# A linear-attention and two-MLP kernel: a new opening order, pairs of units one chunk earlier, a decay written in place, and low halves taken earlier

## The chip, the cores and the metric

One core of one Trainium2 chip runs the whole program in one launch. The metric is the device time of that launch in microseconds (us). TensorE is called PE in the profile (its weight loads PEld), VectorE DVE, ScalarE ACT, GpSimd POOL, SyncE SP. SP issues all DMAs here (SPq in the profile).

## The reference

Inputs are q, k, v and f_logit of shape (4, 8, 768, 48): 4 batches, 8 heads, 768 time steps, 48 features.

```
f = 1 / (1 + exp(-f_logit))
for t in range(768):
    state = f[t][:, None] * state + outer(k[t], v[t])      # 48 x 48 per batch and head
    y[t]  = q[t] @ state
x = y as (3072 tokens, 384)
x = relu(x @ w_in)**2 @ w_out                              # 384 -> 2048 -> 384
h = x @ w_in2 ;  x = (h * tanh(softplus(h))) @ w_out2      # softplus(h) = h above 20
```

All of it is float32.

## The kernel before

**Attention.** Time is cut into 12 pieces of 64 steps, the batches into two pairs: 24 units (`NU`), unit i being piece i // 2 of batch pair i % 2. In a unit the decays are accumulated in log space: `v_min` clips the logits on DVE, `a_exp` and `a_ln` make softplus on ACT, `v_scan` sums along time on DVE, `a_dq` and `a_dk` (ACT) make the queries' and the keys' decay, `v_q` (twice) and `v_k` multiply them in on DVE. Then `m_a` multiplies keys with queries on PE, `v_mask` cuts the result on DVE, `m_t` and `a_kn` turn the keys, `m_y` makes the output, `m_u` and `v_s` the next state, `a_x` and `v_x` split the output into a high and a low part for the MLP (block b of 512 tokens is units 4b to 4b+3). From unit 10 on, units run in pairs: `quarters_a` stands for `m_a` of both, `quarters_u` for `m_u` of the pair before, `v_turn` (DVE) and `a_turn` (8 small copies on ACT) for the turning.

**MLPs.** Each has 6 blocks of 512 tokens and 16 hidden chunks of 128. A float32 product is three fp32r products of high and low parts: `l1` (line 330) is 9 matmuls of 512 columns into one PSUM tile h, `l2` (line 341) 9 matmuls into the three accumulators a0 to a2. Between them ACT takes relu, square and the high half `gh` (`act_a`), DVE the low half `gl` (`act_b`, line 354). At the last chunk of a block `evac` copies the three accumulators out, two on ACT (line 363) and one on DVE (line 361).

**Weights.** They come as 64-bit floats and are rebuilt into float32 halves. For each of the first MLP's 16 chunks `load_w` fetches 768 KB, ACT does `w_abs` and `w_hi`, DVE `w_shift`, `w_top`, `w_low` and `w_lo` (lines 252, 255, 258, 280). The second MLP's weights go the same way beside the middle of the first one (`w2_...`), through DRAM.

**PSUM.** The pool `hps` has five buffers that take turns. `l1`, `m_a`, `m_t`, `m_y`, `m_u` take one each, a `quarters_u` two and a `quarters_a` two. An `l1` can't start before the reader of the tile that had its buffer is done.

**What sets the order.** Instructions stand on their engine in the order in which Python calls them. The opening, up to MLP chunk 18, is a list written out by hand, `START`. It also holds fillers, `m_warm n`, matmuls whose result nobody reads. Behind it a planner sets the order: `put(s, prio, f, ...)` files a step under MLP chunk s, and chunk by chunk the steps are called by rising prio. In a chunk i there are `act_a` of chunk i-1 (5), the attention's steps (9 to 33), `act_b` of i-1 (32 before), `do_l1` of i (100), `quarters_u` and `quarters_a` (110, 111), `do_l2` of i-2 (120). A block's `evac` belongs to the `do_l2` of its last chunk, so it is called in chunks 17, 33, 49, 65 and 81.

**DMA.** SP issues loads in the order of the list and waits at one whose buffer is still in use. Sizes: decay logits alone 256 KB, keys and queries 512 KB, all three 768 KB, values two DMAs of 128 KB, a weight chunk 768 KB. Units 2 to 5 borrow the buffers of weight chunks 15 to 12 for their inputs (`early`).

Of the kernel before, what the change touches and what calls it, by code (L numbers as in the profile page):

```python
# [36 lines left out]
START = """
m_warm 14; load_j 0; v_min 0; a_exp 0; load_j 1; load_j 2; load_j 3; a_ln 0; v_min 1; a_exp 1; v_scan 0; a_ln 1;
load_f 0; load_f 1; v_min 2; v_scan 1; a_dq 0; v_min 3; a_dk 0; v_k 0; a_exp 2; a_dq 1; v_q 0 1; v_q 0 0; a_dk 1;
load_v 0; load_w 0; a_ln 2; a_exp 3; eye_kn 0; load_v 1; load_f 2; m_t 0; m_warm 2; v_end 1; v_k 1; v_q 1 1; load_v 2;  # L40
v_scan 2; a_ln 3; load_f 3; v_end 0; v_q 1 0; m_a 0; m_warm 5; v_scan 3; v_mask 0 0; w_abs 0; v_mask 0 1; m_a 1;
m_warm 4; a_dq 2; a_dk 2; v_mask 1 1; load_v 3; a_dq 3; v_mask 1 0; m_y 0; a_kn 0; load_w 1; w_shift 0; a_dk 3; v_q 2
0; m_t 1; m_warm 2; w_top 0; eye_kn 1; v_q 2 1; load_w 2; m_y 1; m_warm 3; v_q 3 0; v_k 3; v_k 2; v_q 3 1; w_low 0;
a_x 0; m_u 0; a_kn 1; v_s 0 0; m_a 2; w_abs 1; v_x 0; load_w 3; v_mask 2 0; m_u 1; v_s 1 0; v_s 0 1; w_shift 1; m_a 3;
m_t 3; v_mask 2 1; w_hi 0; a_kn 3; m_t 2; m_warm 1; m_y 2; a_kn 2; v_s 1 1; v_mask 3 1; v_mask 3 0; m_warm 1; m_y 3;
m_warm 1; w_lo 0; w_top 1; load_w 4; w_abs 2; a_x 1; v_x 1; w_shift 2; load_f 5; w_low 1; a_x 2; load_w 5; m_warm 6;
load_w 6; v_end 3; a_x 3; v_x 3; v_x 2; w_top 2; do_l1 0; w_hi 1; w_abs 3; load_v 4; w_lo 1; w_low 2; do_l1 1; w_abs
4; w_shift 3; v_min 5; w_hi 2; load_w 7; w_top 3; a_exp 5; w_lo 2; w_shift 4; m_u 3; load_w 8; w_low 3; act_a 0; act_b
0; w_abs 5; w_top 4; w_hi 3; w_shift 5; load_w 9; do_l1 2; act_a 1; w_lo 3; w_low 4; w_hi 4; act_b 1; load_w 11; w_top
5; w_lo 4; w_low 5; v_s 3 0; do_l2 0; do_l1 3; do_l2 1; act_a 2; act_b 2; do_l1 4; w_abs 6; w_hi 5; w_abs 7; w_shift  # L50
6; w_lo 5; w_top 6; do_l2 2; act_a 3; w_abs 8; w_shift 7; w_low 6; load_f 4; a_ln 5; w_hi 6; w_top 7; act_b 3; v_s 3
1; act_a 4; w_lo 6; w_abs 9; do_l1 5; do_l2 3; w_low 7; w_hi 7; load_v 5; act_b 4; w_shift 8; load_f 7; act_a 5;
w_shift 9; load_w 10; do_l1 6; w_top 8; load_f 6; do_l2 4; v_end 2; w_lo 7; w_top 9; w_low 8; act_b 5; act_a 6; w_hi
8; w_abs 11; v_min 4; v_scan 5; w_lo 8; load_v 7; do_l1 7; w_low 9; load_w 14; a_exp 4; do_l2 5; a_ln 4; act_b 6; a_dq
5; w_hi 9; a_dk 5; v_q 5 1; w_abs 10; w_lo 9; v_scan 4; do_l1 8; act_a 7; do_l2 6; v_k 5; a_dq 4; v_q 5 0; act_a 8;
do_l1 9; a_dk 4; w_shift 10; act_b 7; w_top 10; v_q 4 1; m_t 5; v_min 6; w_shift 11; v_k 4; act_a 9; act_b 8; m_a 5;
load_w 12; do_l2 7; v_min 7; m_u 2; v_q 4 0; do_l2 8; w_low 10; a_kn 5; m_a 4; w_top 11; m_t 4; a_exp 7; v_mask 5 0;
w_hi 10; a_ln 7; w_lo 10; v_end 5; v_end 4; w_low 11; act_b 9; w_abs 12; w_hi 11; w_shift 12; v_mask 5 1; w_top 12;
do_l1 10; do_l2 9; w_lo 11; act_a 10; do_l1 11; w_low 12; load_w 13; w_hi 12; w_abs 13; act_b 10; do_l2 10; v_mask 4
1; w_lo 12; v_s 2 0; v_s 2 1; do_l1 12; act_a 11; w_shift 13; v_mask 4 0; w_abs 14; a_exp 6; act_b 11; m_y 5; a_ln 6;  # L60
w_top 13; w_shift 14; a_kn 4; do_l2 11; w_low 13; v_scan 6; w_hi 13; m_y 4; w_lo 13; act_a 12; do_l1 13; v_scan 7;
w_top 14; a_dq 7; act_b 12; a_dk 7; load_w 15; w_low 14; v_q 7 0; m_u 5; v_s 5 0; v_k 7; a_dq 6; v_q 7 1; do_l2 12;
act_a 13; m_u 4; a_dk 6; m_a 7; act_b 13; v_s 4 0; v_q 6 1; w_hi 14; v_q 6 0; do_l2 13; v_s 5 1; load_v 8; v_k 6; v_s
4 1; v_mask 7 1; m_t 7; a_kn 7; w_abs 15; v_mask 7 0; m_a 6; v_mask 6 1; m_t 6; m_y 7; v_mask 6 0; a_kn 6; load_v 6;
a_x 5; m_y 6; a_x 4; w_lo 14; w_shift 15; do_l1 14; v_end 7; w_top 15; w_low 15; v_x 5; load_f 9; w_hi 15; v_x 4;
load_f 8; v_end 6; m_u 7; act_a 14; w_lo 15; m_u 6; v_s 7 0; v_min 8; v_s 7 1; a_exp 8; v_min 9; do_l1 15; a_ln 8; a_x
6; act_b 14; a_x 7; v_scan 8; v_x 6; a_dq 8; v_x 7; v_s 6 1; do_l2 14; a_dk 8; a_exp 9; v_s 6 0; v_k 8; act_a 15; v_q
8 0; act_b 15; a_ln 9; do_l1 16; v_scan 9; m_t 8; v_end 8; act_a 16; load_v 10; do_l1 17; a_dq 9; v_q 8 1; v_q 9 0;
v_end 9; a_dk 9; load_v 9; do_l2 15; a_kn 8; v_q 9 1; do_l1 18; act_b 16; m_a 8; v_mask 8 1; v_mask 8 0; do_l2 16; m_y
8; m_u 8; act_a 17; load_f 10; act_b 17; v_k 9; v_s 8 0; v_s 8 1  # L70
"""
# [880 lines left out]
```

## Time and profile before

| | us |
|---|---|
| median of three runs | 891.13 (889.51 to 891.47) |
| the profiled execution: its time | 892.6 |
| its span, first to last instruction | 890.8 |
| PE busy | 872.1 (98%) |
| DVE busy | 683.9 (77%) |
| ACT busy | 626.6 (70%) |

The granted PE clock is a share of 2.4 GHz; its mean over the span is 0.993. Matmuls are pipelined, so one of 512 columns shows 390 ns while nine of them start within 2.04 us. "Idle before" in a row is the engine's idle time just before it, with what ended it. The span falls into an opening (up to the first `l1` at 38.24 us), the first MLP beside the attention (to about 430 us) and the second MLP.

### The profile page before, as it was taken

What the parts mean: (1) busy time and instruction counts of PE and PEld (TensorE: products, weight loads), DVE (VectorE), ACT (ScalarE), POOL (GpSimd) and SP (SyncE); (2) the same over time, 40 slices, a digit from 0 to 9 for tenths busy, and PEclk for the clock granted to TensorE, in tenths of its full rate; (3) what the DMA queues carried; (4) which work ended last, traced back from release to release, by engine and by line L of the source; (5) the groups of instructions that cost most, each with busy time, mean ns of one, the idle gap of its engine ahead of it and who ended that gap; (6) DMA issues with size and microseconds to landing.
All of it is one profiled execution on the core that took longest, in us unless ns stands there. A gap on an engine that the chain in (4) does not pass through costs nothing.

```text
span 890.8 us, 16582 instructions
## 1 busy us (share of the span) xinstructions
PE 872.1 (98%) x6619; PEld 720.4 (81%) x6619; DVE 683.9 (77%) x1159; ACT 626.6 (70%) x1151; POOL 6.5 (1%) x21
## 2 busy tenths in 40 slices
PE   8899999999999999999999999999999999999996
PEld 8788778887887888788888888888888888888885
DVE  7899986786988897972122888888888888888875
ACT  7598777987987987954544666676666766676664
POOL 2000000000000000000000000000000000000000
PEclk9799999999999999999999999999999999999999
DMA  9962133535466354632653200200200200200001
GB/s 243 387 199 104 51 124 104 181 128 202 147 198 213 131 202 143 202 107 72 212 181 104 71 1 1 71 1 1 71 0 1 71 1 1 71 1 17 20 0 40
DMA packets 30132, 90.80 MB, mean 102 GB/s; under 512 B 3680, under 2 KB 3680, under 8 KB 30048
## 3 DMA queue, kind: packets, MB, share of 16 engines
q1 hardware_dynamic: 30048, 89.67, 30.0%
q8 instruction: 54, 0.88, 0.4%
q14 instruction: 30, 0.25, 0.1%
HBM read 67.63 MB, written 22.02 MB: 101 GB/s over the span
## 4 chain that ended last, share of the span: by engine, by line
PE 83%; DVE 9%; DMA 4%; ACT 2%; issue 1%; SPq 1%; ACTq 0%
PE a L341 40%; PE h L330 40%; DMA r<-in_w_dram 2%; PE y L545 2%; DVE wbit L255 1%; DMA vs<-in_vv_dram 1%; DVE w L280 1%; DVE gl L354 1%; DVE wbit L258 1%; PE aq L478 1%; PE uq L489 1%; DVE vs L571 1%; DVE mv L520 1%; DVE wbit L252 1%; DVE mv L447 0%
## 5 line engine op out<-in xcount | busy, mean ns | idle before, releaser
L330 PE MATMUL h<-x,w 128*128 128x512 f32 x1728 | 424.8, 390 | 3.9 <-ACT r L721 3.5
L341 PE MATMUL a<-gh,w 128*128 128x512 f32 x1146 | 386.4, 392 | 0.0
L330 PEld LDWEIGHTS h<-x,w 128*128 128x128 f32 x1728 | 323.4, 188 | 72.9 <-ACT r L721 4.8
L341 PEld LDWEIGHTS a<-gh,w 128*128 128x128 f32 x1146 | 215.1, 188 | 45.6
L341 PE MATMUL a<-gl,w 128*128 128x512 f32 x573 | 223.4, 390 | 0.5 <-DVE gl L354 0.5
L788 ACT ACTIVATE e<-e 128x512 f32<-128x512 f32 x95 | 60.0, 632 | 116.1 <-DVE e L787 116.1
L341 PEld LDWEIGHTS a<-gl,w 128*128 128x128 f32 x573 | 107.7, 188 | 23.5 <-DVE gl L354 1.8
L354 DVE TENSOR_TENSOR gl<-r,gh 128x512 fp32r<-128x512 f32 x96 | 65.5, 683 | 74.5 <-ACT gh L349 74.0
L787 DVE TENSOR_SCALAR e<-h 128x512 f32<-128x512 f32 x95 | 65.7, 692 | 59.2 <-PE h L330 56.7
L721 ACT ACTIVATE r<-h 128x512 f32<-128x512 f32 x96 | 56.5, 588 | 52.8 <-PE h L330 52.1
L782 ACT ACTIVATE r<-u,cst 128x512 f32<-128x512 f32 x94 | 67.9, 722 | 8.7 <-DVE u L796 2.7
L796 DVE SCALAR_TENSOR_TENSOR u<-e 128x512 f32<-128x512 f32 x95 | 66.0, 694 | 10.0 <-ACT e L788 0.7
L354 DVE TENSOR_TENSOR gl<-g,gh 128x512 fp32r<-128x512 f32 x95 | 65.8, 693 | 0.0
L784 DVE TENSOR_TENSOR e<-h,u 128x512 f32<-128x512 f32 x94 | 64.4, 685 | 0.0
L791 DVE TENSOR_TENSOR g<-e,r 128x512 f32<-128x512 f32 x94 | 64.2, 683 | 0.0
L722 ACT ACTIVATE r<-r 128x512 f32<-128x512 f32 x96 | 60.7, 633 | 3.1
L349 ACT ACTIVATE gh<-r 128x512 fp32r<-128x512 f32 x96 | 60.7, 633 | 3.1
L349 ACT ACTIVATE gh<-g 128x512 fp32r<-128x512 f32 x95 | 60.1, 633 | 3.1 <-DVE g L815 0.8
L783 ACT ACTIVATE r<-r 128x512 f32<-128x512 f32 x94 | 59.4, 632 | 3.0
L500 ACT ACTIVATE kn<-kt 32x256 f32<-32x256 f32 (+1 forms) x104 | 37.6, 362 | 1.4
L432 DVE TENSOR_TENSOR_SCAN es<-es,cap 112x520 f32<-112x520 f32 x24 | 29.6, 1232 | 0.8 <-ACT es L428 0.8
L447 DVE TENSOR_TENSOR mv<-in,eq 48x512 f32<-48x512 f32 x40 | 27.4, 685 | 1.4 <-ACT eq L437 0.6
(116 smaller groups left out, 679.7 us busy)
## 6 DMA issues: line engine op xcount, KB each, us to landing
in<-in_qkf_dram SPq DMA_DIRECT2D x18, 768.0 KB, 6.7
r<-in_w_dram SPq DMA_DIRECT2D x16, 768.0 KB, 10.6
sr<-in_w_dram SPq DMA_DIRECT2D x32, 384.0 KB, 3.7
w2d<-sw SPq DMA_DIRECT2D x32, 384.0 KB, 3.7
w<-w2d SPq DMA_DIRECT2D x32, 384.0 KB, 3.6
vs<-in_vv_dram SPq DMA_DIRECT2D x48, 128.0 KB, 7.3
x2d<-ot SPq DMA_DIRECT2D x18, 256.0 KB, 2.2
x<-x2d SPq DMA_DIRECT2D x6, 768.0 KB, 5.1
```

The lines of the kernel that those rows point to most:

```text
L330: T.matmul(out=ps, lhsT=w[:, k * 128:(k + 1) * 128], rhs=x[:, s, k], start=(i == 0), stop=(i == 8))
L341: T.matmul(out=acc[m], lhsT=w[:, m * 128:(m + 1) * 128], rhs=gx, start=(fc == 0 and i == 0), stop=(fc == FC - 1 and i == 2))
L349: A.activation(out=gh, in_=g, func=AF.Copy)
L354: V.tensor_tensor(out=gl, in0=g, in1=gh.bitcast(F32), op=ALU.subtract)
L722: A.activation(out=r, in_=r, func=AF.Square)
L782: A.activation(out=r, in_=u, func=AF.Ln, bias=two)
L783: A.activation(out=r, in_=r, func=AF.Exp, scale=-1.0)
L784: V.tensor_tensor(out=e, in0=hp, in1=u, op=ALU.mult)
L787: V.tensor_scalar(out=e2, in0=ps, scalar1=20.0, scalar2=None, op0=ALU.min)
L788: A.activation(out=e2, in_=e2, func=AF.Exp)
L791: V.tensor_tensor(out=g, in0=e, in1=r, op=ALU.mult)
L796: V.scalar_tensor_tensor(out=u2, in0=e2, scalar=2.0, in1=e2, op0=ALU.add, op1=ALU.mult)
```

## The change

- `START` is a new list. The step names are the same; their order on every engine, and that of the loads on SP, differs.
- `m_warm n` makes matmuls of up to 512 columns: n counts 128 columns each, as before, but four go into one instruction.
- `a_dq` writes the queries' decay over the unit's decay logits, which `a_exp` has read by then, and no longer into a tile of its own (`eq`).
- Pairs from unit 12 on start one chunk earlier (s is one less), while `m_y`, `a_x` and `v_x` keep their chunk (`end`). `v_s` moves one chunk earlier for all pairs.
- `act_b` has priority 20 in place of 32 outside the last block: ahead of `v_min` (24), `v_scan` (25), `v_q`, `v_k`, `v_end` (26), `v_turn` (27).

```diff
-m_warm 14; load_j 0; v_min 0; a_exp 0; load_j 1; load_j 2; load_j 3; a_ln 0; v_min 1; a_exp 1; v_scan 0; a_ln 1;
+m_warm 20; load_j 0; v_min 0; a_exp 0; load_w 0; load_j 1; load_j 2; a_ln 0; v_scan 0; w_abs 0; v_min 1; a_dq 0;
...
         def a_dq(i):
-            eq = at.tile([112, H, C], F32, tag="eq", name="eq")
+            eq = head(fkq(i)[0])
             A.activation(out=eq, in_=es[i % 3][:, :, 1:], func=AF.Exp, scale=-1.0)
...
         def m_warm(n):
             sm = cap.rearrange("p h t -> p (h t)")
-            for _ in range(n):
-                T.matmul(out=warm[:, 0:128], lhsT=sm[:, 0:128], rhs=sm[:, 0:128])
+            for k in range(n, 0, -4):
+                c = 128 * min(k, 4)
+                T.matmul(out=warm[:, 0:c], lhsT=sm[:, 0:128], rhs=sm[:, 0:c])
...
-                end = s + 4
+                end = 8 * (i // 2) - 11
...
-                    put(s + 9, 12 - odd, v_s, i, 0)
-                    put(s + 10, 9 - odd, v_s, i, 1)
+                    put(8 * (i // 2) - 7, 12 - odd, v_s, i, 0)
+                    put(8 * (i // 2) - 6, 9 - odd, v_s, i, 1)
...
-                s = 8 * (i // 2) - 16 + i % 2
+                s = 8 * (i // 2) - (17 if i > PAIRS + 1 else 16) + i % 2
...
-                put(i, 17 if i > last else 32, act_b, i - 1)
+                put(i, 17 if i > last else 20, act_b, i - 1)
```

On PE, near the end of block 1 (accumulators a_1722 before, a_1748 after), the pair of units 12 and 13 stood ahead of the block's last `l2`. L489 is `quarters_u`, L478 `quarters_a`. Before:

```order
L330 MATMUL h<-x,w_526 128x512 x9
L341 MATMUL a_1722<-gh,w_1383 128x512
...
L330 MATMUL h<-x,w_651 128x512 x9
L489 MATMUL uq<-vs_152,kn_156 48x48 x16
L489 MATMUL uq<-vs_153,kn_157 48x48 x16
L478 MATMUL aq<-mv_154,in_144 64x64 x16
L478 MATMUL aq<-mv_155,in_145 64x64 x16
L341 MATMUL a_1722<-gh,w_1530 128x512
...
L330 MATMUL h<-x,w_673 128x512 x9
```

And after (each line number is one or two higher):

```order
L331 MATMUL h<-x,w_359 128x512 x9
L490 MATMUL uq<-vs_152,kn_156 48x48 x16
L490 MATMUL uq<-vs_153,kn_157 48x48 x16
L479 MATMUL aq<-mv_154,in_144 64x64 x16
L479 MATMUL aq<-mv_155,in_145 64x64 x16
L342 MATMUL a_1748<-gh,w_1382 128x512
...
L331 MATMUL h<-x,w_448 128x512 x9
L342 MATMUL a_1748<-gh,w_1426 128x512
...
L331 MATMUL h<-x,w_640 128x512 x9
```

The four groups now stand behind the `l1` of chunk 32, not 33; the block's last `l2` (w_1530 before, w_1426 after) has one plain chunk ahead of it.

On ACT at the same place, L363 (L364 after) is the eviction, L721 to L349 (L723 to L350) one `act_a`, L500 (L501) the `a_turn` of unit 12. Before:

```order
L349 ACTIVATE gh<-r 128x512
L363 ACTIVATE ot<-a_1722 128x512
L363 ACTIVATE ot<-a_1724 128x512
L721 ACTIVATE r<-h 128x512
L722 ACTIVATE r<-r 128x512
L349 ACTIVATE gh<-r 128x512
L500 ACTIVATE kn_156<-kt_164 32x8x32 x2
```

After:

```order
L350 ACTIVATE gh<-r 128x512
L501 ACTIVATE kn_156<-kt_164 32x8x32 x2
L501 ACTIVATE kn_156<-kt_164 32x8x16 x2
...
L364 ACTIVATE ot<-a_1748 128x512
L364 ACTIVATE ot<-a_1750 128x512
L723 ACTIVATE r<-h 128x512
```

The eight turning copies went ahead of the eviction.

On SP, at the very start, the loads of the opening: `in` and `early` are inputs of units 0 to 3 (144 to 147) and 4, 5 (148, 149), `vs` values, `r` raw weights (r_255, r_377, r_393, r_480 are chunks 0 to 3 before; r_211, r_234, r_401, r_309 after). Before:

```order
L405 DMA in_145<-in_qkf_dram 128x1024
L417 DMA vs_150<-in_vv_dram 64x512 x2
L239 DMA r_255<-in_w_dram 128x1536
L417 DMA vs_151<-in_vv_dram 64x512 x2
L405 DMA early_146<-in_qkf_dram 128x1024
L417 DMA vs_152<-in_vv_dram 64x512 x2
L405 DMA early_147<-in_qkf_dram 128x1024
L417 DMA vs_153<-in_vv_dram 64x512 x2
L239 DMA r_377<-in_w_dram 128x1536
L239 DMA r_393<-in_w_dram 128x1536
```

After:

```order
L240 DMA r_234<-in_w_dram 128x1536
L406 DMA early_147<-in_qkf_dram 128x512
L418 DMA vs_150<-in_vv_dram 64x512 x2
L406 DMA early_146<-in_qkf_dram 128x1024
L406 DMA early_149<-in_qkf_dram 128x1536
L240 DMA r_309<-in_w_dram 128x1536
L418 DMA vs_151<-in_vv_dram 64x512 x2
L406 DMA early_147<-in_qkf_dram 128x1024
L240 DMA r_401<-in_w_dram 128x1536
L418 DMA vs_152<-in_vv_dram 64x512 x2
L418 DMA vs_153<-in_vv_dram 64x512 x2
```

Weight chunks 0, 1, 3 and 2 and the input of unit 5 now stand ahead of the values of units 2 and 3. Ten places further on, the input of unit 4 (early_148) comes ahead of chunks 6, 11 and 7.

## Rows read from the trace of the kernel before

**Rows 1.** The page: busy us, share of the span, instructions.

```profile
PE 872.1 (98%) x6619; PEld 720.4 (81%) x6619; DVE 683.9 (77%) x1159; ACT 626.6 (70%) x1151; POOL 6.5 (1%) x21
```

**Rows 2.** Stretches: us, busy us (instructions) by engine, clock, DMA share, GB/s.

```profile
38.00:130.00 92.00, 90.74 (x916) 72.86 (x914) 89.80 (x130) 77.32 (x149) 0.00 (x0) 1.00 0.40 135
130.00:200.00 70.00, 70.00 (x717) 57.26 (x716) 51.45 (x103) 56.82 (x119) 0.00 (x0) 1.00 0.45 145
200.00:400.00 200.00, 196.15 (x2167) 160.89 (x2166) 167.50 (x331) 161.96 (x346) 0.00 (x0) 1.00 0.51 171
```

**Rows 3.** PE's waits, 130 to 450 us: us in total, times, longest.

```profile
PE h L330 <- ACT r L721: 3.5, 3, 1.2
PE a L341 <- DVE gl L354: 0.3, 1, 0.3
```

**Rows 4.** Timeline of PE at an eviction: start, us, what [idle before].

```profile
352.10 0.94 PE L489 MATMUL uq<-vs,kn 64*48 64x48 f32 x64
...
353.91 0.50 PE L341 MATMUL a<-gh,w 128*128 128x512 f32 x1
...
357.43 2.34 PE L330 MATMUL h<-x,w 128*128 128x512 f32 x9 [1.17 <-ACT r L721]
```

**Rows 5.** Timeline of ACT beside rows 4.

```profile
354.91 0.60 ACT L363 ACTIVATE ot<-a 128x512 f32<-128x512 f32 x1 [3.78 <-PE a L341]
356.29 0.60 ACT L363 ACTIVATE ot<-a 128x512 f32<-128x512 f32 x1 [0.79 <-PE a L341]
356.79 0.59 ACT L721 ACTIVATE r<-h 128x512 f32<-128x512 f32 x1
```

**Rows 6.** Timeline of PE behind a pair without an eviction.

```profile
241.89 0.50 PE L341 MATMUL a<-gh,w 128*128 128x512 f32 x1
...
244.06 2.20 PE L330 MATMUL h<-x,w 128*128 128x512 f32 x9
```

**Rows 7.** Stretches, columns as rows 2, cut where DVE changes.

```profile
3.50:39.10 35.60, 31.11 (x565) 28.34 (x564) 29.71 (x45) 23.59 (x52) 4.01 (x10) 0.86 1.01 317
39.10:115.90 76.80, 76.08 (x818) 61.35 (x820) 75.80 (x107) 63.38 (x121) 0.00 (x0) 1.00 0.43 147
```

**Rows 8.** Timeline at the last weight chunk: DVE's last step.

```profile
115.94 0.96 DVE L280 SCALAR_TENSOR_TENSOR w<-wbit,w 128x768 fp32r<-128x768 f32 x1 [0.32 <-ACT w L275]
```

**Rows 9.** Timeline of PE there.

```profile
116.78 2.34 PE L330 MATMUL h<-x,w 128*128 128x512 f32 x9
```

**Rows 10.** DVE's waits, 3 to 39.1 us, the longest.

```profile
DVE x L585 <- ACT x L581: 1.1, 1, 1.1
...
DVE es L432 <- ACT es L428: 0.8, 1, 0.8
```

**Rows 11.** Timeline of SP, 27.1 to 27.3 us: the load of weight chunk 7.

```profile
27.14 0.33 SPq L239 DMA_DIRECT2D r<-in_w_dram  x1
```

**Rows 12.** That DMA: KB, us from issue to landing.

```profile
r<-in_w_dram SPq DMA_DIRECT2D x1, 768.0 KB, 14.0
```

**Rows 13.** Stretches of the opening, columns as rows 2: weights alone, values between.

```profile
22.50:33.00 10.50, 7.61 (x112) 6.75 (x106) 9.01 (x15) 3.64 (x9) 0.00 (x0) 0.61 1.01 416
9.50:22.00 12.50, 11.59 (x261) 10.44 (x262) 11.61 (x16) 9.36 (x21) 0.00 (x0) 1.00 1.04 251
```

**Rows 14.** Timeline of PE in the opening: five fillers, and its longest wait.

```profile
13.00 1.38 PE L592 MATMUL warm<-cap 112*128 112x128 f32 x10
...
24.54 0.27 PE L466 MATMUL at<-mv,early 48*64 48x64 f32 x1 [1.93 <-DVE early L451]
```

**Rows 15.** The page's groups: line, operation, count | busy us, mean ns | idle before.

```profile
L432 DVE TENSOR_TENSOR_SCAN es<-es,cap 112x520 f32<-112x520 f32 x24 | 29.6, 1232 | 0.8 <-ACT es L428 0.8
L447 DVE TENSOR_TENSOR mv<-in,eq 48x512 f32<-48x512 f32 x40 | 27.4, 685 | 1.4 <-ACT eq L437 0.6
```

**Rows 16.** DVE's waits for the high half, whole span.

```profile
DVE gl L354 <- ACT gh L349: 74.0, 34, 4.2
```

**Rows 17.** The stretch behind the wait of rows 14, columns as rows 2.

```profile
24.90:35.10 10.20, 8.93 (x166) 8.07 (x161) 8.72 (x14) 4.79 (x12) 0.00 (x0) 0.50 1.02 412
```

More of the change, by code (lines that the diff above doesn't have):

```diff
@@ L37 @@
 START = """
-m_warm 14; load_j 0; v_min 0; a_exp 0; load_j 1; load_j 2; load_j 3; a_ln 0; v_min 1; a_exp 1; v_scan 0; a_ln 1;
[L39 to L67, printed above, removed]
@@ L68 @@
-8 0; act_b 15; a_ln 9; do_l1 16; v_scan 9; m_t 8; v_end 8; act_a 16; load_v 10; do_l1 17; a_dq 9; v_q 8 1; v_q 9 0;
-v_end 9; a_dk 9; load_v 9; do_l2 15; a_kn 8; v_q 9 1; do_l1 18; act_b 16; m_a 8; v_mask 8 1; v_mask 8 0; do_l2 16; m_y
-8; m_u 8; act_a 17; load_f 10; act_b 17; v_k 9; v_s 8 0; v_s 8 1
+m_warm 20; load_j 0; v_min 0; a_exp 0; load_w 0; load_j 1; load_j 2; a_ln 0; v_scan 0; w_abs 0; v_min 1; a_dq 0;
+a_exp 1; w_shift 0; v_min 2; w_top 0; load_f 0; a_ln 1; load_f 1; v_scan 1; a_dk 0; a_exp 2; v_q 0 0; v_k 0; a_dq 1;
@@ new lines @@
+load_w 1; v_q 0 1; v_q 1 0; a_dk 1; m_a 0; v_k 1; a_ln 2; eye_kn 0; v_q 1 1; m_warm 3; m_a 1; v_mask 0 0; load_j 3;
+m_t 1; load_v 0; v_scan 2; v_mask 1 1; v_min 3; a_dq 2; w_abs 1; load_f 2; w_low 0; a_dk 2; m_t 0; v_mask 0 1;
+v_end 1; load_f 5; v_mask 1 0; w_shift 1; v_k 2; load_w 3; load_v 1; a_exp 3; a_ln 3; a_kn 1; m_warm 9; m_y 0;
+eye_kn 1; v_end 2; w_hi 0; load_f 3; m_warm 13; m_y 1; v_q 2 1; w_top 1; load_w 2; v_scan 3; w_low 1; v_q 2 0; a_x 0;
+a_dq 3; load_v 2; v_x 0; m_warm 2; m_a 2; a_x 1; load_v 3; w_lo 0; a_kn 0; v_min 5; a_dk 3; v_q 3 0; v_k 3; v_end 0;
@@ new lines @@
+v_end 3; v_mask 2 0; v_mask 2 1; w_hi 1; w_abs 2; m_u 0; a_exp 5; v_q 3 1; m_warm 3; m_t 3; v_x 1; v_s 0 1; m_warm 5;
+m_a 3; v_s 0 0; m_t 2; m_u 1; m_y 2; v_mask 3 1; w_abs 3; load_v 4; w_shift 2; w_shift 3; a_kn 3; v_mask 3 0; a_x 2;
+v_s 1 1; load_w 5; a_ln 5; v_s 1 0; a_kn 2; m_warm 5; m_y 3; v_x 2; w_top 2; a_x 3; load_w 8; load_w 4; load_f 4;
+w_top 3; v_x 3; w_lo 1; w_abs 4; w_low 2; m_warm 6; do_l1 0; v_min 4; w_shift 4; w_low 3; w_hi 2; act_a 0; w_lo 2;
+do_l1 1; w_top 4; act_b 0; w_hi 3; w_low 4; m_u 2; w_abs 5; act_a 1; w_shift 5; load_w 6; load_w 11; w_lo 3; do_l1 2;
@@ new lines @@
+w_hi 4; w_top 5; load_w 7; w_lo 4; act_b 1; do_l2 0; w_abs 6; v_scan 5; do_l1 3; act_a 2; v_s 2 0; act_a 3; w_shift 6;
+do_l2 1; act_b 2; w_low 5; do_l1 4; act_b 3; a_dq 5; load_w 15; w_abs 7; load_w 10; load_f 7; load_v 5; w_top 6;
+w_hi 5; a_dk 5; a_exp 4; a_ln 4; v_s 2 1; load_w 9; w_lo 5; do_l2 2; do_l1 5; m_u 3; act_a 4; v_k 5; w_low 6; w_abs 8;
+v_scan 4; m_t 5; load_v 6; w_hi 6; w_shift 7; act_b 4; w_top 7; a_dq 4; act_a 5; w_lo 6; w_abs 9; do_l2 3; w_low 7;
+w_shift 8; a_dk 4; v_s 3 0; w_top 8; act_b 5; a_kn 5; w_hi 7; do_l2 4; w_low 8; do_l1 6; w_lo 7; w_hi 8; do_l2 5;
@@ new lines @@
+do_l1 7; load_f 6; v_q 4 1; act_a 6; w_lo 8; v_q 5 1; act_b 6; w_abs 10; w_shift 9; v_q 5 0; v_s 3 1; do_l2 6;
+w_abs 11; v_k 4; w_top 9; m_t 4; w_shift 10; do_l1 8; load_w 14; w_low 9; act_a 7; act_b 7; v_end 5; v_q 4 0; w_hi 9;
+m_a 5; act_a 8; a_kn 4; w_lo 9; w_top 10; v_min 7; w_low 10; v_min 6; v_mask 5 0; do_l2 7; do_l1 9; w_hi 10; m_a 4;
+w_shift 11; v_mask 5 1; v_end 4; load_w 12; act_a 9; w_lo 10; act_b 8; a_exp 7; m_y 5; a_exp 6; v_mask 4 1; do_l1 10;
+a_ln 7; w_top 11; w_abs 12; a_x 5; act_b 9; load_w 13; do_l2 8; a_ln 6; w_low 11; w_shift 12; w_hi 11; m_u 5;
@@ new lines @@
+v_scan 7; v_mask 4 0; do_l2 9; v_x 5; w_top 12; w_lo 11; w_low 12; w_abs 13; w_shift 13; act_a 10; a_dq 7; m_y 4;
+do_l1 11; w_abs 14; act_b 10; w_top 13; w_hi 12; do_l2 10; w_lo 12; w_low 13; act_a 11; a_dk 7; do_l1 12; w_hi 13;
+act_b 11; v_s 5 0; w_lo 13; v_end 7; v_q 7 1; v_s 5 1; v_k 7; act_a 12; do_l2 11; a_x 4; do_l1 13; v_scan 6; a_dq 6;
+v_x 4; m_t 7; act_b 12; a_dk 6; load_v 7; v_q 7 0; w_shift 14; do_l2 12; v_k 6; m_t 6; w_top 14; act_a 13; v_end 6;
+act_b 13; a_kn 7; m_a 7; do_l2 13; w_low 14; m_u 4; v_q 6 1; w_hi 14; v_q 6 0; w_lo 14; load_f 9; w_abs 15;
@@ new lines @@
+w_shift 15; m_a 6; do_l1 14; v_mask 7 0; v_mask 7 1; a_kn 6; w_top 15; v_s 4 0; w_low 15; w_hi 15; v_s 4 1; act_a 14;
+m_y 7; load_f 8; v_mask 6 0; v_mask 6 1; a_x 7; w_lo 15; m_u 7; load_v 9; v_min 8; m_u 6; v_min 9; a_exp 8; m_y 6;
+v_s 6 0; act_b 14; a_ln 8; v_scan 8; a_exp 9; a_x 6; v_x 6; do_l1 15; v_x 7; a_ln 9; do_l2 14; v_s 7 0; a_dq 8;
+v_s 7 1; a_dk 8; v_k 8; v_s 6 1; v_scan 9; do_l1 16; act_a 15; v_end 8; m_t 8; v_q 8 1; act_a 16; load_v 8; a_dq 9;
+a_kn 8; do_l1 17; load_v 10; v_q 8 0; a_dk 9; act_b 15; m_a 8; act_b 16; v_q 9 1; v_mask 8 1; v_k 9; v_mask 8 0;
@@ L71 @@
+act_a 17; load_f 10; v_q 9 0; do_l2 15; m_u 8; m_y 8; act_b 17; v_s 8 0; do_l1 18; v_s 8 1; a_x 8; v_end 9; v_x 8;
+do_l2 16
 """
```

## The prediction

> **What bounds the kernel now.** I read the page first: PE is busy for 872.1 of 890.8 us [rows 1], so only its waits and what makes it late can be won. The stretches say where. From 130 to 200 us PE never stops; from 38 to 130 it is idle for 92.00 - 90.74 = 1.26 us, from 200 to 400 for 3.85 us [rows 2]. The view of waits names the second figure: three waits of an `l1` for ACT, 3.5 us together, and one of 0.3 us for `gl` [rows 3]. So there are two places: the opening with the stretch behind it, and those three waits.
>
> The three waits. Behind the quarters of a pair PE runs an `l2` and then stands for 1.17 us [rows 4]. On ACT at that time the two evictions end at 354.91 + 0.60 and 356.29 + 0.60 us, each having waited for PE's `l2`, and only then comes the relu of the chunk before [rows 5]. `l1` needs that relu: five PSUM buffers take turns, the quarters took four, so the next `l1` gets the buffer of the previous one. Where the quarters meet no eviction, `l1` follows without a wait [rows 6]. They meet in chunks 33, 49 and 65, the three times of [rows 3].
>
> The opening. The first nine matmuls of the MLP start at 38.24 us, but DVE is what sets the pace behind them: from 39.10 to 115.90 us it is busy for 75.80 of 76.80 us [rows 7], and its `w_lo` of the last weight chunk, from 115.94 to 116.90 us with a wait of 0.32 us ahead of it [rows 8], is what the `l1` that starts at 116.78 needs [rows 9]. Before 39.10 DVE was idle for 35.60 - 29.71 = 5.89 us. PE's time at 117 us is thus DVE's work up to that `w_lo` plus DVE's idle time, 5.89 + 1.00 = 6.9 us.
>
> **The change part by part.** *Pairs one chunk earlier.* Quarters now stand in chunks 32, 48 and 64, evictions still in 33, 49 and 65. From the `l2` behind the quarters to the next `l1` it is 357.43 - 353.91 = 3.52 us where they meet and 244.06 - 241.89 = 2.17 us where they don't, a difference of 1.35 us, of which 1.17 is the wait and the rest the restart. Three times that is 4.05 us. What could come late next: in chunk 33 ACT now has `act_a`, eight turning copies and the evictions, so the relu of chunk 33 still waits for the eviction, but the `l1` behind it takes the buffer of the first state quarter, which the earlier `v_s` has read by then, about 4 us before. The high half of chunk 34 comes closest: some 1 us before its `l2` by my count of ACT's work, and it is the place where the wait of 0.3 us stands now. I take -4.0 us, with bounds of -4.4 (that wait goes too) and 0 (the wait only moves).
>
> *Opening order.* Counting the steps of both lists up to `w_lo` of the last weight chunk gives DVE the same work: 8 clips, scans and key products, 16 query products and masks, 12 state updates, 6 output splits, 16 of each weight step, 14 low halves. So this `w_lo` moves by the change of DVE's idle time alone. What DVE waits for in the new order: at the start the first scan follows the first clip at once, so it has the 0.8 us of [rows 10] and the 0.6 us that the second clip had filled, 1.4 us; the first weight step waits for `w_abs` of a load that now comes second on SP, some 0.5 to 1 us; the keys' decay of unit 3 stands on ACT behind the output of unit 1, some 0.5 us. These two are estimates, set beside the 0.8 and 1.1 us that DVE lost to ACT before [rows 10]. The 1.1 us at the last split [rows 10] goes, since two weight steps (0.96 us in [rows 8]) stand before it and give ACT time.
>
> The large question is a load. `v_min 4` now stands two weight steps behind the last split, and unit 4's input is the 27th DMA. Up to it SP moves 11.3 MB (11264 KB: four units of logits, keys and queries, five of values, seven weight chunks, two whole inputs). Before, weight chunk 7 was the 27th and closed the same 11264 KB; it landed at 27.14 + 14.0 = 41.1 us [rows 11, 12]. The mix is the same to one load, and the DMA engines were saturated (share 1.01 and 1.04 in [rows 13]), so it lands at about 41 us. DVE gets there at 3.5 us plus its work so far: that of [rows 7] up to the last split, 29.7 us, plus what the new list does more by then, a clip, a `w_shift`, two `w_top` and two weight steps behind the split, some 4.3 us, plus the waits above, 2.4 to 2.9 us, and small gaps: 40 to 41 us. So this wait is worth 0 to 1.5 us. All idle time comes to about 2.9 + 0.7 + 0.7 for small gaps (the 1.0 us of the stretch to 115.90 less its named wait) = 4.3 us in place of 6.9. I take -2.6 us; the bounds are -5 us (DVE is never kept waiting but at the start) and +1 us (the loads come 2 us later and the keys of unit 3 with them).
>
> The rate decides this. A weight chunk alone moves at 416 GB/s and anything with values at 251 [rows 13]. The Trainium skill (DMA: Bandwidth & Descriptors, Specifications) gives a limit of about 358 GB/s from HBM for one core. The trace exceeds it; by the page's figure each of seven weight chunks would take 2.2 us in place of 1.9 and the sum would be about 2 us worse, and the measured rate is used.
>
> *Fillers.* Behind the front block there are 46 units of 128 columns in place of 25. Five took 1.38 us [rows 14], so 46 take 12.7 us, 5.8 more than 25. Each group stands ahead of a step that waits for DVE or for a load, which is what hides it at full clock. I take 0, with 5.8 us as the upper bound, all of it in the way, and at half clock see below.
>
> *Decay in place.* No instruction is added; `v_end` now has to be done before the unit's input is overwritten, but that load waits for `v_q` and the keys' products anyway, which come with or after it. 0, bounds of 0.2 us each way.
>
> *`gl` earlier.* It moves ahead of a chunk's preparation, up to a scan of 1.23 us and four steps of 0.69 us [rows 15], which covers the 0.3 us wait of [rows 3] with its restart: -0.4 us. What it costs is a wait for `gh` before the attention's preparation; DVE idles 74 us for that in all [rows 16], but is busy for only 167.5 of 200 us in [rows 2] and the preparation is due a chunk later. Some small new waits: +0.2 us, bounds 0 and +2.
>
> Sum: -4.0 - 2.6 - 0.4 + 0.2 = -6.8 us. From the profiled 892.6 that is 885.8 us; that execution lies 1.5 us above the median of the three runs, so I forecast 884.3 us.
>
> **The rivals.** *The opening gives nothing.* For it: it is bound by loads, and they are the same bytes. Against it: DVE's waits there were for ACT more than for loads, the two longest at least [rows 10]. Then 891.1 - 4.2 = 886.9 us.
>
> *The wait only moves.* The change doesn't do what it says if the `l1` of chunk 34 waits for a quarter's reader that stands behind the eviction on DVE. For it: five buffers remain. Against it: in the new order the first `v_s` stands ahead of the eviction. Then 891.1 - 2.8 = 888.3 us.
>
> *The clock falls again.* After PE's idle 1.93 us [rows 14] the granted clock was 0.50 for 10.2 us, that is 1.2 GHz [rows 17]. If PE waits as long for the values of unit 1, which now land behind three weight chunks, the 22 filler units around `m_y 0` and `m_y 1`, and 10 more before the last key product, run at half speed: 32 x 0.28 = 9.0 us more of PE work, about half of it behind the last input and in the way. DVE loses some 4.5 us: 891.1 - 4.2 + 4.5 = 891.4 us, no change or slower. The Trainium skill (TensorE: Matmul & The Clock Gate, Why this matters for your kernels) warns of idle gaps between bursts of matmuls for this reason, and the trace agrees with that fall; it also speaks for the fillers.
>
> *`gl` holds up the pairs; slower.* Place: DVE in the chunks before each of the seven pairs from unit 10 on. The wait for `gh` is 2.2 us on average, 4.2 at most [rows 16]; the preparation behind it lasts up to 1.23 + 4 x 0.69 = 4.0 us [rows 15], a chunk on PE some 4.3 us, twice the 2.17 us of [rows 6]. If DVE waits the average in two chunks running, it is 2 x (2.2 + 4.0 - 4.3) = 3.8 us late, of which the slack of half a chunk takes 2.2; 1.6 us per pair, seven times, is 11 us: 884.3 + 11 = 895 us. It decides from the point where wait and work exceed the chunk; with 16% of DVE free in [rows 2] one such chunk is taken up by the next.
>
> **How the numbers follow.** The forecast has 0.60, its own range 881 to 886.5. The opening without gain 0.18, the wait that moves 0.06, the clock 0.08, `gl` 0.08. Changes within 0.2% (1.8 us) can't be told from none. Faster: the first three, 0.84. The clock case is the same or slower by halves, 0.04 each; `gl`, by how many pairs it catches, the same with 0.03 and slower with 0.05: 0.07 and 0.09 in all. The range is 880.8 (an opening with the full 5 us and the lower bounds elsewhere) to 889.3 (the wait that moves and an opening 1 us short of the rival's).
>
> **What would show it.** In the profile after: no wait of an `l1` for ACT's relu beyond 0.3 us; 2.2 us from the `l2` behind the quarters to the next `l1` everywhere; the last `w_lo` some 2.6 us earlier than 115.94, with DVE's idle time ahead of it near 4.3 us; the clip of unit 4 waiting for its load up to about 41 us; a granted clock of 1.00 in the opening. It is wrong if the first MLP's last weight step isn't earlier, if a wait for relu remains, or if quarters wait for DVE.

## The result, and the profile after

The changed kernel takes 903.9 us (median of 4 runs, 903.62 to 903.98), the kernel before 890.94 us beside it. The ratio is 1.0147 (95% interval 1.013 to 1.0165): slower by 13 us, where 884.3 us was forecast, with a range of 880.8 to 889.3.

The stretches of [rows 2] and [rows 7] in the profile after (us, busy us by engine, granted clock, DMA share, GB/s); the span is 902.2 us:

```profile
38.00:130.00 92.00, 90.20 (x936) 73.38 (x934) 87.07 (x125) 74.46 (x142) 0.00 (x0) 0.98 0.37 129
130.00:200.00 70.00, 68.07 (x677) 55.11 (x676) 43.09 (x87) 50.34 (x106) 0.00 (x0) 1.00 0.39 124
200.00:400.00 200.00, 191.76 (x2134) 156.32 (x2133) 167.52 (x327) 164.68 (x355) 0.00 (x0) 0.99 0.51 173
3.50:39.10 35.60, 33.57 (x516) 21.25 (x515) 33.06 (x50) 25.25 (x56) 4.48 (x10) 1.00 0.89 330
39.10:113.50 74.40, 74.40 (x787) 60.71 (x786) 72.89 (x103) 62.10 (x118) 0.00 (x0) 1.00 0.42 146
```

From 130 to 200 us PE never stopped before; now it is idle for 1.93 us, and from 200 to 400 for 8.24 in place of 3.85. The waits of PE from 130 to 450 us, in the place of [rows 3]:

```profile
PE h L331 <- ACT r L723: 3.4, 2, 1.7
PE aq L479 <- DVE in L452: 2.8, 5, 0.9
PE aq L479 <- ACT r L723: 1.5, 1, 1.5
PE y L546 <- DVE mv L518: 1.3, 2, 1.1
PE a L342 <- DVE gl L355: 1.1, 2, 0.8
```

The named waits grew from 3.8 to 10.1 us. Quarters (`aq`) now wait for the keys' product on DVE (L452), the output `y` for the mask, and an `l1` still waits for relu. On ACT two waits of the same stretch grew with them, on DVE one:

```profile
ACT in L438 <- DVE es L433: 24.6, 14, 3.8
ACT sw L304 <- DVE wbit L259: 14.2, 6, 4.1
```

```profile
DVE gl L355 <- ACT gh L350: 54.7, 24, 4.2
```

Before, the same three were:

```profile
ACT eq L437 <- DVE es L432: 8.3, 9, 3.1
ACT sw L303 <- DVE wbit L258: 3.3, 2, 1.9
```

```profile
DVE gl L354 <- ACT gh L349: 45.0, 24, 4.2
```

The first is `a_dq`, the exponential behind the scan; the second the high half of a weight of the second MLP.

Where the time goes is seen best in the start of each `l1`, taken from the traces as the profiled execution less that of the kernel before, in us. Each is one execution, and the one of the kernel before lies 1.5 us above its median, so the columns tell the place of a loss better than its size. "Early" and "cut" are explained below:

| kernel | l1 15 | l1 20 | l1 30 | l1 42 | l1 58 | l1 75 |
|---|---|---|---|---|---|---|
| changed | 0.0 | +1.1 | +3.7 | +9.1 | +9.1 | +11.6 |
| changed, `gl` late | +0.3 | +1.4 | +1.4 | +1.2 | +0.1 | -0.7 |
| changed, pairs back | +0.5 | +1.6 | +2.5 | +7.6 | +10.6 | +11.1 |
| before, `gl` early | -0.7 | -0.8 | +0.1 | +9.0 | +10.0 | +10.8 |
| before, pairs early | -1.0 | -1.0 | -1.0 | -1.5 | -2.5 | -2.0 |
| before, new opening | +0.3 | +1.4 | +1.4 | +1.3 | +1.3 | +1.3 |
| changed, loop cut | +0.5 | +1.6 | +1.6 | +1.1 | 0.0 | -0.8 |
| changed, `gl` late, states later | -1.9 | -0.6 | -0.6 | -1.1 | -2.2 | -3.0 |

The changed kernel loses 1.1 us by chunk 20 and 10.5 beside the attention, chunks 25 to 75; behind that nothing changes. Not all of the 10.5 us is waiting: from 130 to 400 us PE's idle time grew by 1.93 + 8.24 - 3.85 = 6.3 us, and behind two of the new waits (1.51 and 0.89 us, ahead of the quarters at 203.42 and 205.00 us) the granted clock falls as well. The ten microseconds around them, before and after:

```profile
200.00:210.00 10.00, 8.83 (x158) 6.97 (x157) 6.00 (x13) 5.20 (x11) 0.00 (x0) 1.00 0.45 156
200.00:210.00 10.00, 7.60 (x145) 5.92 (x144) 9.78 (x20) 8.33 (x20) 0.00 (x0) 0.83 0.52 169
```

A mean of 0.83 over 10 us costs about 1.7 us of PE's work.

### The profile page after: what moved, and what is told of

Read it like the earlier page. It is cut to its first block, busy times and chain, and to the rows that moved or that the text cites. A ratio compares the mean times of both kernels' runs of the same rounds, so it can differ in the third digit from the quotient of the medians.

```text
span 902.2 us, 16454 instructions
## 1 busy us (share of the span) xinstructions
PE 878.9 (97%) x6563; PEld 715.1 (79%) x6563; DVE 684.8 (76%) x1159; ACT 626.5 (69%) x1151; POOL 7.0 (1%) x21
## 4 chain that ended last, share of the span: by engine, by line
PE 70%; DVE 13%; ACT 11%; issue 3%; DMA 3%; SPq 0%; DVEq 0%; ACTq 0%
PE h L331 32%; PE a L342 31%; PE warm L594 2%; DVE gl L355 2%; DVE es L433 2%; ACT r L724 2%; ACT gh L350 2%; ACT r L723 1%; DVE wbit L256 1%; PE y L546 1%; DMA sr<-in_w_dram 1%; DVE mv L448 1%; ACT wbit L249 1%; ACT kn L501 1%; DMA in<-in_qkf_dram 1%
## 5 line engine op out<-in xcount | busy, mean ns | idle before, releaser
L723 ACT ACTIVATE r<-h 128x512 f32<-128x512 f32 x96 | 56.5, 588 | 57.8 <-PE h L331 57.5
L350 ACT ACTIVATE gh<-r 128x512 fp32r<-128x512 f32 x96 | 60.8, 633 | 3.1
L350 ACT ACTIVATE gh<-g 128x512 fp32r<-128x512 f32 x95 | 60.2, 634 | 3.1 <-DVE g L817 0.8
L501 ACT ACTIVATE kn<-kt 32x256 f32<-32x256 f32 (+1 forms) x104 | 37.6, 362 | 1.4
L438 ACT ACTIVATE in<-es 112x512 f32<-112x512 f32 x20 | 12.6, 631 | 25.8 <-DVE es L433 25.8
## 6 DMA issues: line engine op xcount, KB each, us to landing
r<-in_w_dram SPq DMA_DIRECT2D x16, 768.0 KB, 10.8
```

Of the source, the lines that this page charges most:

```text
L350: A.activation(out=gh, in_=g, func=AF.Copy)
L723: A.activation(out=r, in_=ps, func=AF.Relu)
```

## The experiments

**Theory A: a loop of DVE and ACT.** At priority 20 `gl` stands on DVE ahead of the next scan and waits there for `gh`. The scan comes late; ACT, which works in order, waits for the scan in `a_dq` and so can't make the next relu and `gh`; DVE then waits for that `gh` with the next `gl`. One turn of it in the changed kernel, DVE and then ACT (start, us, what, idle before):

```profile
158.43 0.69 DVE L355 TENSOR_TENSOR gl<-r,gh 128x512 fp32r<-128x512 f32 x1 [3.12 <-ACT gh L350]
159.04 1.23 DVE L433 TENSOR_TENSOR_SCAN es<-es,cap 112x520 f32<-112x520 f32 x1
160.31 1.39 DVE L448 TENSOR_TENSOR mv<-in 48x512 f32<-48x512 f32 x2
161.62 0.68 DVE L452 TENSOR_TENSOR in<-in,es 112x512 f32<-112x512 f32 x1
162.22 0.35 DVE L460 TENSOR_TENSOR fmin<-fmin,f 112x8 f32<-112x8 f32 x2
164.52 0.69 DVE L355 TENSOR_TENSOR gl<-r,gh 128x512 fp32r<-128x512 f32 x1 [1.95 <-ACT gh L350]
```

```profile
157.76 0.63 ACT L350 ACTIVATE gh<-r 128x512 fp32r<-128x512 f32 x1
158.30 0.20 ACT L456 ACTIVATE f<-in 112x8 f32<-112x8 f32 x1
160.31 0.64 ACT L438 ACTIVATE in<-es 112x512 f32<-112x512 f32 x1 [1.81 <-DVE es L433]
160.97 0.63 ACT L443 ACTIVATE es<-es 112x512 f32<-112x512 f32 x1
...
162.59 0.57 ACT L723 ACTIVATE r<-h 128x512 f32<-128x512 f32 x1
163.19 0.63 ACT L724 ACTIVATE r<-r 128x512 f32<-128x512 f32 x1
163.85 0.63 ACT L350 ACTIVATE gh<-r 128x512 fp32r<-128x512 f32 x1
```

DVE idles 3.12 us for `gh`, runs the scan, and ACT has idled 1.81 us for it; the next `gh` starts 6.1 us after the last one, where a chunk takes 4.1, and DVE idles again. Theory B was that pairs a chunk earlier took the slack away, theory C that the opening leaves the loss behind.

*`gl` late* (`gl_late`):

```diff
-                put(i, 17 if i > last else 20, act_b, i - 1)
+                put(i, 17 if i > last else 32, act_b, i - 1)
```

> The changed kernel (903.9 us) with `act_b` of the chunks beside the attention back at priority 32, behind the preparation; the rest of the change stays. Theory A (the early `gl` stands ahead of the scan on DVE, waits there for `gh`, and ACT, which waits for the scan, then brings the next `gh` late): the loss beside the pairs goes, 886 to 890 us, and DVE's waits of `gl` for `gh` fall from 97 us to about 75. Theory B (a chunk less for the pairs took the slack away): still 900 to 904. Theory C (the new opening leaves the loss): 902 to 904.

890.2 us, ratio to before 0.9992 (0.998 to 1.0003), at the upper end of what theory A gave. The loss beside the pairs is gone; of PE's waits from 130 to 450 us one line is left:

```profile
PE a L342 <- DVE gl L355: 1.2, 2, 0.6
```

*Pairs back* (`pairs_back`): the diff's lines on `end`, `v_s` and `s` undone, `gl` early.

> The changed kernel with the pairs' quarters and their `v_s` back in the chunks that they had before; `gl` stays early. Theory A (early `gl`): most of the loss stays, 897 to 903 us. Theory B (pairs a chunk earlier): 890 to 892. If both are needed for the loss: 890 to 893 here and 886 to 890 with `gl` late.

903.84 us, ratio 1.0155 (1.012 to 1.0189). B falls: with `gl` early it makes no difference where the pairs stand.

*`gl` alone* (`gl_alone`): before with 20 for 32.

> The kernel before (890.9 us) with `act_b` at priority 20 and nothing else of the change. Theory A: 898 to 904 us, with ACT's exponentials of the queries' decay waiting for the scan by some 20 us in all (9.3 before). Theory B and theory C: 890 to 892.

902.84 us, ratio 1.0122 (1.0098 to 1.0146); ACT waits 23.8 us for the scan from 130 to 450 us. C falls as well: this one line does nearly all of it.

*Pairs alone* (`pairs_alone`): before with the diff's lines on the pairs (they move those from unit 12 on; the expectation says 14).

> The kernel before with the pairs from unit 14 on a chunk earlier and their `v_s` moved with them as in the change, and nothing else. Theory A, with the prediction's own term for the pairs: 886 to 888 us, the waits of `h` for ACT's relu (3 of 1.17 us) gone. Theory B: 899 to 904. Theory C: 886 to 891.

888.13 us, ratio 0.997 (0.9958 to 0.9982): faster by 2.7 us by the ratio, 3.1 by the medians. No `l1` waits for relu, but `l2` now waits for `gl`:

```profile
PE a L341 <- DVE gl L354: 2.0, 3, 1.2
```

Is it the scan in ACT's queue, or any work behind DVE's wait (rival A2)? Two runs ask that.

*Behind the scan* (`gl_behind_scan`): the changed kernel, `act_b` at 25.5.

> The changed kernel with `act_b` at priority 25.5 in place of 20: behind the clip and the scan of a unit, still ahead of its queries' and keys' products. Theory A as it stands (the scan queued behind `gl` is what keeps ACT from `gh`): most of the loss goes, 889 to 893 us. Rival A2 (any work of the preparation queued behind `gl` is late by DVE's waits for `gh`, scan or not): 896 to 902.

895.34 us, ratio 1.0049 (1.0024 to 1.0075). Between the two: 8.6 of the 13.7 us that a late `gl` gives back. The keys' product is still behind the wait (`aq` waits 0.9 us for it, two `l1` 0.8 for relu). PE's named waits come to 3.6 us against 1.2 with `gl` late; the rest of the 5.1 us between these two kernels isn't traced.

*Loop cut* (`loop_cut`): the changed kernel, `gl` early, the waiting work of ACT moved behind its `gh`.

```diff
-            put(s - 2, 32, a_dq, i)
-            put(s - 2, 32, a_dk, i)
+            put(s - 1, 6, a_dq, i)
+            put(s - 1, 6, a_dk, i)
```

> The changed kernel with `gl` still at priority 20, but the two exponentials that wait for the scan (`a_dq`, `a_dk`) moved into the next chunk, behind that chunk's relu, square and `gh` on ACT. Theory A (the loop of DVE and ACT): `gh` no longer stands behind a wait for the scan, relu comes in time, and the time is 888 to 894 us. Rival A2 (DVE's waiting alone makes the preparation late): 897 to 904, with quarters still waiting for the keys' product.

891.5 us, ratio 1.0009 (0.9991 to 1.0027): 12.4 of the 13.7 us come back with `gl` still early. PE's waits and ACT's for the scan, 130 to 450 us:

```profile
PE a L342 <- DVE gl L355: 1.2, 2, 0.9
PE aq L479 <- DVE in L452: 0.2, 1, 0.2
```

```profile
ACT in L438 <- DVE es L433: 1.1, 2, 0.5
```

DVE waits for `gh` as long as in the changed kernel (56.1 us in all against 54.7), so its waiting alone costs at most the 1.3 us that are left by the medians; A2 falls as the main cause. What costs is the wait of ACT inside the loop.

**Theory F: PE without instructions in the opening.** The theory is that PE runs out of issued instructions there. The last `w_lo` did come early, and yet `l1` 15 did not (changed kernel; DVE, then PE, then the stretch behind it):

```profile
113.51 0.96 DVE L281 SCALAR_TENSOR_TENSOR w<-wbit,w 128x768 fp32r<-128x768 f32 x1
```

```profile
113.61 1.08 PE L546 MATMUL y<-mv,vs 112*32 112x64 f32 x58
116.50 0.31 PE L546 MATMUL y<-mv,vs 128*32 128x64 f32 x6 [1.80 <-issue]
116.74 3.58 PE L331 MATMUL h<-x,w 128*128 128x512 f32 x9
```

```profile
117.00:121.00 4.00, 4.00 (x12) 3.10 (x12) 3.92 (x8) 2.72 (x6) 0.00 (x0) 0.57 0.12 37
```

Fifty-eight of the 64 matmuls of unit 6's output run, then PE stands for 1.80 us with no semaphore to wait for, and the granted clock is 0.57 over the next 4 us, mostly the level of 1.2 GHz. (The Trainium skill, TensorE: Matmul & The Clock Gate, Why this matters for your kernels, warns of idle gaps between bursts of matmuls, though of longer ones; here the lower clock followed one of 1.80 us.) The new list calls `m_y 7`, `m_u 7`, `m_u 6` and `m_y 6` one after the other; 186 of their 192 small matmuls, each with its own weight load, run within 4 us ahead of that wait.

*New opening alone* (`opening_alone`): before with the new list, fillers and decay.

> The kernel before (891.2 us) with the new order of the opening, its fillers of 512 columns and the queries' decay over its inputs; pairs and `gl` as before. The prediction's own term: 888.3 us (-2.6). Theory F (in the opening PE has 186 small matmuls begun within 4 us, runs out of issued instructions before the last six of unit 6's output, waits 1.8 us for no semaphore, and its clock falls behind that): the last low half of the weights is 2.4 us earlier and yet the time is 892 to 893.5, with that wait of 1.6 to 2.0 us in the trace near 116.5.

892.89 us, ratio 1.0019 (1.0008 to 1.0031), with that wait at 1.95 us, as theory F had it.

*States later* (`u_later`): the changed kernel, `gl` late, and in the list:

```diff
-w_lo 15; m_u 7; load_v 9; v_min 8; m_u 6; v_min 9; a_exp 8; m_y 6; v_s 6 0; act_b 14; ... v_x 6; do_l1 15; v_x 7; a_ln 9; do_l2 14; v_s 7 0;
+w_lo 15; load_v 9; v_min 8; v_min 9; a_exp 8; m_y 6; act_b 14; ... v_x 6; do_l1 15; m_u 7; m_u 6; v_x 7; a_ln 9; do_l2 14; v_s 6 0; v_s 7 0;
```

> The changed kernel with `gl` late (890.2 us) and, in the opening's list, `m_u 7`, `m_u 6` and `v_s 6 0` behind `do_l1 15`, so that nine matmuls of 512 columns stand between unit 6's output and the states. Theory F: the wait without a semaphore ahead of the last matmuls of unit 6's output goes or falls below 0.5 us, the granted clock stays 1.00 over 117 to 121 us, and the time is 886.5 to 888.5. Rival G (unit 6's output waits for a mask or a load whose record the trace doesn't tie to it): the wait of 1.8 to 2.0 us stays, 889.5 to 890.5.

889.09 us, ratio 0.9988 (0.9975 to 1.0001), so 1.1 us less by the medians; in the traces `l1` 15 comes 2.2 and `l1` 20 2.0 us earlier. The wait without a semaphore is gone and the clock stays; 0.74 us of an ordinary wait takes its place. The time lies between F's range and G's; the trace decides for F:

```profile
113.67 1.33 PE L546 MATMUL y<-mv,vs 112*32 112x64 f32 x64 [0.74 <-ACT w L276]
114.93 2.33 PE L331 MATMUL h<-x,w 128*128 128x512 f32 x9
```

```profile
117.00:121.00 4.00, 4.00 (x76) 3.38 (x75) 3.85 (x7) 3.90 (x9) 0.00 (x0) 1.00 0.13 37
```

**Both mended** (`both_mended`): `gl` early with the loop cut, states later.

> The changed kernel with both faults mended: `gl` early, but the two exponentials that wait for the scan behind the next chunk's `gh` on ACT, and the states of units 6 and 7 behind `do_l1 15` in the opening. If the two mends add up (loop cut alone 891.5, states later 1.1 to 2.3 us off): 887 to 889.5, at or below the 889.1 of the late `gl` with the states later, because the waits for `gl` ahead of its matmuls shrink. If an early `gl` is worth nothing even without the loop: the same 889 to 890.

888.92 us, ratio 0.9984 (0.9975 to 0.9993). The mends add up (903.9 - 12.4 - 1.1 = 890.4 us, and it came out 1.5 us lower), but an early `gl` gains nothing that these times can tell: with it late the time was 889.09 us.

**Decay and fillers, priced by themselves.** The first try put both into the old opening with early pairs (`pairs_decay_fillers`), and the same with the early, cut `gl` (`old_opening_cut`).

> The kernel before with the pairs a chunk earlier, the queries' decay over its inputs and the fillers of 512 columns, in the old order of the opening and with `gl` late. The prediction's terms for the last two (nothing each): 887.5 to 889, as with the pairs alone (888.1). If one of them is what the opening lost (2.0 us): 889.5 to 891.

> The run with pairs, decay and fillers in the old opening, and on top the early `gl` with the scan's two exponentials behind the next `gh`. If the early `gl` pays once the loop is cut: 886 to 887.5, with the waits of `a` for `gl` (2.2 us with the pairs alone) below 1.3. If not: 887.5 to 889.5.

899.94 and 899.78 us. In both, the old list loads unit 8's inputs before unit 6's last decay is copied from the same place, so the factor of unit 6's state is read from wrong data, and ACT waits 3.9 and 4.7 us for that load. They price neither edit. With `v_end 6` ahead of `load_f 8` (`pairs_decay_swap`, `old_opening_cut_swap`):

> Pairs a chunk earlier, decay over its inputs and fillers of 512 columns in the old opening, `gl` late, and in the list `v_end 6` ahead of `load_f 8` (in the run before, unit 6's last decay was copied from a place that unit 8's load had overwritten). If decay and fillers cost nothing, as predicted: 887 to 889 (pairs alone 888.1), ACT's wait of 3.88 us for that load gone. If the fillers or the decay shift the opening against PE's supply of instructions: 890 to 893, with waits for no semaphore ahead of unit 6's or 7's output.

> The same with `gl` early and the scan's two exponentials behind the next `gh`. If an early `gl` pays once the loop is cut: 0.4 to 1.5 us under the run beside it, the waits of `a` for `gl` shorter. If not: within 0.4 us of it.

900.99 and 901.22 us, ratios 1.0116 (1.0097 to 1.0134) and 1.0128 (1.0113 to 1.0144): a miss again, with `l1` 20 later than before by 13.3 and 8.6 us. So each edit was run alone on the kernel before.

> The kernel before with the queries' decay over its inputs, and `v_end 6` ahead of `load_f 8` in the list (otherwise unit 6's last decay would be read from unit 8's inputs); nothing else. The prediction: 890 to 891. If the loads of the later units, which now wait for the copy of the last decay, come late for the clip at the head of DVE's queue: 896 to 901, with DVE's clip waiting 3 to 5 us for the load near 125 us.

900.9 us, ratio 1.0111 (1.0095 to 1.0127). SP's waits from 10 to 130 us hold two that before lacks, for the copy of the last decay on ACT (L455), and DVE's clip then waits for the load:

```profile
SPq L405 <- ACT f L455: 6.9, 2, 4.8
...
SPq L239 <- ACT f L455: 6.1, 1, 6.1
```

```profile
DVE in L421 <- DMA in<-in_qkf_dram: 5.1, 1, 5.1
```

L239 is a weight load: units 2 to 5 sit in the buffers of weight chunks 15 to 12. Whatever else SP has to load waits behind. `fillers_alone`:

> The kernel before (890.4 us) with fillers of 512 columns in place of four of 128 and nothing else. The prediction: 890 to 891. If the fewer instructions ahead of unit 0's output move PE's supply of instructions into the loads (theory F): a wait for no semaphore of about 3 us ahead of unit 0's output at 20 to 24 us, and 890 to 893, since the loads bound that stretch anyway.

895.65 us, ratio 1.0055 (1.0039 to 1.0071), above both forecasts, with the wait that theory F names:

```profile
23.95 0.44 PE L545 MATMUL y<-mv,vs 128*32 128x64 f32 x6 [4.44 <-issue]
```

The profiled execution (892.6 us) is 3 us shorter than the other three (895.4 to 896.7), so its trace can't show where most of the price arises. In the new opening (`small_fillers`, the changed kernel with `gl` late and fillers of 128 columns):

> The changed kernel with `gl` late (890.2 us) and the fillers back to one instruction for each 128 columns. The prediction: 889.5 to 891, fillers hidden either way. If the number of instructions on PE decides when its supply runs out (theory F): the waits for no semaphore (0.9 us near 36.5, 2.0 near 116.9) change place and size, and the time moves by more than 1.5 us, to either side.

890.71 us, ratio 0.9998 (0.9988 to 1.0008): no difference there, where F had expected more than 1.5 us. The waits for no semaphore did move, as F has it: 1.9 us near 37.8 and none near 117, in place of 0.9 and 2.0. The lower clock moved along (0.50 from 37.8 to 41.2 us, and 1.00 from 117 to 121), and the last `w_lo` came 2.5 us later, at 116.23 us in place of 113.72. Here the 192 small matmuls of `m_y 7`, `m_u 7`, `m_u 6` and `m_y 6` run one after the other without a wait, so that they stand together isn't enough for one; how many instructions came before decides too.

**What was worth keeping** (`pairs_gl_cut`): before with early pairs and an early `gl`, loop cut.

> The kernel before with pairs a chunk earlier, `gl` at priority 20 and the scan's two exponentials behind the next `gh`; opening, decay and fillers as before. If an early `gl` pays once the loop is cut: 886.5 to 888, under the pairs alone (888.1). If it is worth nothing: 888 to 889. If cutting the loop needs the decay over its inputs (its own tile has fewer buffers): above 890.

888.19 us, ratio 0.9972 (0.9959 to 0.9985), equal to the pairs alone. These two are the fastest, 0.3% under the kernel before; both mended is 0.16% under it.

## Why the prediction was wrong

- *`gl` earlier, -0.4 and +0.2 (0 to +2).* This step failed: it measured +11.6 us alone and +13.7 in the changed kernel. The working argued from DVE's free time, "busy for only 167.5 of 200 us in [rows 2] and the preparation is due a chunk later". DVE is as busy after, 167.52 us of the same 200. What it left out is who waits for the scan: ACT, in order, with the next relu and `gh` behind it. The working itself names the scan ([rows 15]) among the steps that `gl` moves past, but quotes no row of ACT's waits for it, 8.3 us in the kernel before and 24.6 after.
- *The rival "`gl` holds up the pairs"* had the place, the sign and about the size (11 us), but got 0.08, and its mechanism was half right. It counted DVE's lateness against the chunk; the run with the loop cut has the same waits of DVE and loses 1.3 us by the medians. The quarters did wait for DVE, which the prediction had named as a sign of being wrong.
- *Pairs a chunk earlier, -4.0 (-4.4 to 0).* Mechanism right, size too large: -2.7 us alone (0.9958 to 0.9982). The three waits of [rows 3] went; 2.0 us of waits for `gl` came, of the kind that the step had named as next, but ahead of the `l2` of chunks 29, 33 and 61 and not of chunk 34. With an early `gl` the gain is nothing, 903.84 against 903.9.
- *Opening, -2.6 (-5 to +1).* On DVE it was right: the last `w_lo` came 2.43 us earlier, with (35.60 - 33.06) + (74.40 - 72.89) = 4.05 us of idle time ahead of it, forecast 4.3; the clip of unit 4 started at 39.93 us, forecast 40 to 41, without a wait, for its load had landed at 29.68 + 9.6 = 39.3 us and not at 41. It did not reach PE: 1.80 us of standing without a semaphore and the clock behind that gave it back. With the decay and the fillers it cost 2.0 us alone. The step followed DVE's queue to the end and put PE's own supply of instructions at nothing.
- *Granted clock of 1.00 in the opening.* Right up to 39 us, wrong at 117 us. The clock rival had the mechanism and the wrong gap, a wait for values.
- *Decay, 0 ± 0.2.* Its reason was wrong: in the old order the load does wait longer, for a copy on ACT, and this costs 10 us. The new list calls `v_end 6` ahead of `load_f 8`, and SP's waits up to 130 us name no such copy there; but in the new order the edit was not priced alone, only within the opening's 2.0 us.
- *Fillers, 0.* Measured 0 in the new opening; in the old one they cost 4.8 us. The waits for no semaphore change with them, but that these make up the 4.8 us is not shown.
- *Sum.* Pairs 0, opening with decay and fillers about +1 to +2, `gl` +11.6: this accounts for the 13.0 us to within about 1 us, what the medians leave open. (The lower bounds of the prediction's terms add up to 881.1 us, not to its 880.8; nothing hangs on it.)

## What to carry to other kernels

A wait on one engine is free only if nothing behind it is what another in-order engine waits for on its way to ending that wait; before moving a waiting instruction forward, list what it overtakes, who waits for that, and whether the chain comes back. Idle share says nothing on this: DVE's, from 200 to 400 us, was the same before and after. When a list is reordered, read every engine's queue and not only the one that sets the pace, and price an edit that frees a buffer later by all the loads that stand behind it on the issuing queue.

## What the runs showed of the hardware

That PE ran out of instructions is read from the times of their packets. The profile's page after lists a DMA queue for instructions (packets, MB, share):

```profile
q8 instruction: 53, 0.87, 0.4%
```

These packets have 16 KB each. In the changed kernel one began at 113.80 us and ended at 115.09; PE resumed at 116.50, 1.41 us later. Other waits of this kind end the same way: packet over at 34.93 and PE on at 36.36 in the changed kernel, 22.40 and 23.95 with the fillers alone, 25.51 and 27.00 before. In all the traces of this case the lag is 1.2 to 1.6 us for each such wait of 0.7 us or more; some shorter ones, as the 0.58 us up to 24.69 us in the changed kernel, don't show it. No semaphore in the trace ties packet and wait, and the trace doesn't say which engine a packet is for. Each wait came amid short matmuls with weight loads of their own, and more or fewer instructions elsewhere moved it. The Trainium skill (Runtime: NRT & Kernel Launch, Instruction fetch mechanics) states that an engine fetches its instructions in blocks of 16 KiB while it executes the block before, and that this is mostly hidden. The size agrees with these packets, and so does "mostly": of eleven that began from 3 to 130 us in the changed kernel, two were followed by a wait of 0.8 us or more. Those that were not hidden cost 0.8 to 4.4 us at a time.
